# Two heads on one core: x transposed out of DRAM, state columns in chunk order

## The chip, the cores and the metric

The kernel runs on one core of a Trainium2 chip. The time is device microseconds of one execution; a kernel's time is the median of several. The profiled execution is one more run of the same program, with the hardware profiler on. Its *span* is the time from the first to the last instruction that the profile shows; the device time has about two microseconds more around it.

## The reference

Two independent parts read two inputs of 2048 tokens by 448 features (bf16); their outputs stand side by side in one array of 2048 x 896.

```
# A: dilated local attention, 16 heads of 28, window 8, dilation 2
q, k, v = split(x @ wqkv)                      # per head
idx     = pos[:, None] - 2 * arange(8)         # masked where negative
logits  = (q . k[idx]) * 28 ** -0.5
a       = (softmax(logits) . v[idx]) @ wo

# B: diagonal state model, 448 complex states
Bu = x @ B_bar.T                               # B_bar from Lambda, log_dt, B_re, B_im
h  = Lam_bar * h + Bu[t]                       # over t = 0 .. 2047
b  = 2 * real(h @ Cmat.T) + x * Dskip
out = concatenate([a, b], -1)
```

## The kernel before

All work is written as small operations (Python functions marked `@op`), and the string ORDER (lines 32 to 61) lists them one by one: this fixes the order on every engine by hand. A name is followed by its arguments; `@` gives the PSUM banks it takes; `.` means that its copy out of PSUM goes to ScalarE, `=` to VectorE. Capital names are mostly TensorE work (QS, QK, V_, BU, BR, UP, H_, DN, C, W_, AV, AL), small ones copies, vector work and DMA issues. Nearly all DMAs are issued by SyncE, in the order in which they stand in the program, so one that waits holds up all behind it.

**Layout.** TensorE contracts over partitions, so x is needed with features on partitions. 448 features are three full blocks of 128 and a half block of 64. The half blocks of two groups of tokens share one tile, one in partitions 0 to 63 and one in 64 to 127, and their two matmuls of half height run side by side. `part` (line 238) issues such a group: six matmuls of full height (k=0) or two of half height (k=1).

**Part A.** The tile `xT` holds x transposed: group 0 has tokens 0 to 1023, group 1 the rest, each as two halves of 512 tokens in seven blocks (three, the shared half block, three). Group 0 is loaded as rows into `xnA`, a view of `xbuf` (lines 141 to 144); TensorE transposes it with an identity (XI for tokens 0 to 511, XA and XH for 512 to 1023), and the copies xi, xa and xh bring it from PSUM into `xT`. Group 1 is loaded as rows too (line 157), in an order of columns that makes two token tiles fill seven whole blocks, and transposed by four DMAs from SBUF to SBUF (line 173). Weights come in slices (w_load, and w_half for the 64 rows of the half block). QS and QK make q and k, V_ makes v. P multiplies q with shifted k on VectorE, E_ sums heads on TensorE, lt copies the sums, TD transposes them by DMA, sma/smb/smc are the softmax. AL, ad and sp lay the weights out in a band (through DRAM), AV multiplies by v, W_ by wo, w copies the result into one of six `ya` buffers, ow stores it.

**Part B.** T=4 steps make a chunk, 512 chunks in all; chunks are of two kinds, even and odd. Rows of B_x are loaded early into `xnB` (x_load, line 164), again with shuffled columns, each quarter cb holding 128 chunks of one kind. xt(cb) transposes a quarter from SBUF to SBUF into `xTB`, which is `xbuf` again, once its A rows are done with. So columns of `xTB` stand sorted by kind: first all even chunks, then all odd ones. XR then loads B_x once more in plain order for the skip term. Bn holds B_re and B_im, BD transposes it into BT. BU multiplies; its sums for step j stay in PSUM, BR adds the rotated state of step j-1 (from the tile Z) on top of them, and z copies the sum to Z, or for the last step only the even half to Z3. UP adds the even chunks' end to the odd chunks', y copies that; sa, sb and sd run the scan over pairs of chunks; DN, H_ and their additions dn and h bring the scan's result back to each step, C multiplies by the output matrix, c adds the skip term and oc stores.

**Around the start.** WU warms TensorE with 22 small matmuls on zeros. SyncE issues the loads of lines 141 to 179 one after another, then what ORDER names.

Of the kernel before, what the change touches and what calls it, by code (L numbers as in the profile page):

```python
# [32 lines left out]
WU@0 XI0@0 xi00= xi01. XI1@1 XI2@2 xi10= xi11. PP@3 xi20. pcopy pa QS00@4 pb QS10@5 qk000. pd_ pc XH1@6 pe XA10@7  # L33
xh1. XA11@1 qk010. xa10= QK021@32 xa11. QK031@04 P000 ty0 QS01@6 pf QS11@5 P001 QK051@71 QK030 tf0 qk011. qk001. pg
ts00 QK050 qk031. ts10 ts20 QK020 qk051. P010 qk050. ty5 V_010@56 ty2 tf5 qk020. QK061@41 P011 V_001@73 ts05 V_011
V_000 v010. qk030. tf2 ts15 QK060 qk021= ts25 v000. P020 v001. QK040@50 qh001. rb2 v011. qh011. QK041 V_111@27 ty1
P021 V_101@36 V_110 qk040. qk041. tf1 ts02 E_00@50 P030 E_01 ts01 ts12 E_02 qh000. V_100 P031 qh010. v111. P040
QK130@41 ts22 ts11 v101. P041 v100. V_411@76 ts21 QK131 E_03 hc0 P050 ty6 E_04 ty4 V_410 qk131. tf6 qk130. QK100@31
P051 v411. ts06 v410. P060 QK110@46 ts16 BD v110. ts26 P061 QK101 ty3 QK151@72 QK111 qk100. E_05 rb0 qk101. E_06
qk110. QK150 tf4 lt00 P100 V_401@31 qk151. V_501@45 V_500 rb3 qk150. xt1 ts04 P101 lt01 QK120@27 ts14 qk111. tf3  # L40
v501. QK140@06 xt0 v500. P110 ts03 QK121 P111 QK141 qk120. QK161@54 V_400 qk140. xt3 P120 ts13 qk121. QK160 v400.
P121 qk141. v401. E_10@20 xt2 ts23 P130 E_11 ts24 V_510@73 qh101. P131 qh110. qh111. E_12 TD0 qh100. P140 E_13 hc1
V_511 P141 v511. v510. LC BU301@61 BU201@45 P150 BU300 sma0 BU200 OZ z30. XR BU400@37 z20. P151 smb0 BU000@64 P160
BR31 P161 BU001 ci1. BU401 E_14 z00. E_15 ci2= CD1 z40. E_16 rb1 z31. BR21 BR01 lt11 BU500@63 ci0= CD2 z21. smc0
z01. BU211@10 ci3. CD0 BU311@54 BU501 BU310 lt10 z50. CD3 BR32 BR41 BU210 z41. xd3 TD1 z32. BR51 xd2 BR22 AL0@2 z51.
BR33 z22. BU100@67 al0= z33. xd0 ca3 ad0 BU011@53 BU111@12 BU101 sma1 OP pm3 BU010 z10. pm0 wo UP3 AL1@6 cs3 smb1
BR11 xd1 BR02 BU110 z02. smc1 z11. BR03 al1. BR12 BU510@57 z03. ad1 z12. pm1 sp0 ca6 UP0 BR13 BU600@61 z13. y3. y0.
cs6 UP1 BR23 BU601 y1. z23. BU511 sa0 BU411@43 z60. BR52 pm4 ca1 BU410 sp1 sb0 BR61 z52. BR42 BU611@26 ca2 BU610 pm2
sd0 z61. AX@5 z42. BR53 BR62 AL2@1 ax= z53. z62. cs1 DN0@4 UP5 adx UP2 al2. DN1@5 BR43 dn0 BR63 y2. dn1 AL3@2 ad2
z63. sa2 H_10@1 y5. H_20@4 z43. H_11@0 al3. UP6 UP4 H_21@5 y6. H_00@7 ad3 y4. H_01@2 AV011@6 ca4 h21 spx AV010@3 h20  # L50
AV030@5 h01 av011. sp2 AV000@4 av010. cs2 AV020@6 av030. sb2 AV021@2 av000. AV001@3 av020. AV031@5 sd2 av001. W_00@4
sp3 av031. av021. W_20@6 ca5 h11 DN2@3 W_01@5 h00 DN3@2 dn2 w20. W_10@0 dn3 w01. sa4 ow20 W_11@7 ow01 W_21@3 w11.
w10. H_03@6 h10 H_02@2 w00. H_22@5 cs4 W_30@7 w21. ow00 sb4 H_23@0 ow21 H_13@1 w30. W_31@4 ow10 ca0 ow30 h13 AV100@3
ow11 h03 AV110@7 sd4 AV111@1 av110. AV131@6 av111. AV101@7 h02 av131. AV121@1 sa6 av101. AV130@6 av121. AV120@2 cs0
av130. DN5@7 av100. cs5 W_71@1 av120. dn5 W_61@6 w31. sb6 w71. h23 H_05@3 ow31 W_51@2 w61. ow71 ow61 W_41@7 w51= h05
H_15@4 ow51 H_25@1 W_50@0 h15 sd6 DN4@6 W_60@2 w50. w41. W_40@3 ow50 w60= ow41 DN6@4 C32@0 w40. ow60 dn6 dn4 ow40
h25 H_06@7 H_16@2 H_04@3 h06 H_12@4 H_14@6 h04 W_70@1 c32 H_24@7 C31@3 h22 oc32 w70= h12 C33@0 ow70 c31 h14 oc31
H_26@5 C30@1 c33 h26 oc33 h24 C02@4 c30 oc30 C20@3 c02 C00@6 c20 h16 oc20 CH0@0 c00 C01@5 oc00 C11@7 c01 ch0 oc01
C12@1 oh0 oc02 C13@4 C22@3 C03@2 c22 c12 oc22 c13 C21@6 oc12 c11 oc13 oc11 C10@5 c21 c03 oc21 CH1@0 oc03 c10 ch1
oc10 oh1  # L60
# [3 lines left out]
def kernel(  # L64
# [48 lines left out]
    def evict(e, o, i):  # L113
        (ACT.copy if e == "A" else V.tensor_copy)(o, i)  # L114
# [45 lines left out]
    xnB = keep.tile([128, 4, T, D], BF16, tag="xnB")  # L160
    xP = xnB.rearrange("p c j d -> p c (j d)").rearrange("p c (a n) -> p c a n", a=2)
    xB_r = B_x[0].rearrange("(q p h a b) d -> h p q a b d", q=2, p=128, h=2, a=2)

    def x_load(hh):
        for d0, d1, b, c in ((0, D, 0, 0), (D, 512, 1, 384), (512, 896, 1, 0)):
            for q in range(2):
                SP.dma_start(xP[:, 2 * hh + q, :, d0:d1], xB_r[hh, :, q, :, b, c:c + d1 - d0])
# [122 lines left out]
    @op  # L290
    def xi(h, k, e):
        p, c = pp["xi", h], 256 * h
        if h == 2:
            evict(e, xT[0:64, 0, 3], p[0:64, 0:512])
        elif k == 0:
            evict(e, xT[:, 0, 0:2, c:c + 256], p[:, 0:512].rearrange("p (f n) -> p f n", f=2))
        else:
            evict(e, xT[:, 0, 2, c:c + 256], p[:, 512:768])

    @op  # L300
    def XA(b, part):
        p = pp["xa", b, part] = ps(BF16)
        for t in range(4):
            for k, f in enumerate((0, 1) if part == 0 else (2,)):
                PE.transpose(p[:, 512 * k + 128 * t:512 * k + 128 * t + 128], xnA[:, 4 * b + t, 128 * f:128 * f + 128], ident[:])

    @op
    def xa(b, part, e):
        p = pp.pop(("xa", b, part))
        if part == 0:  # L310
            evict(e, xT[:, 0, 4 * b:4 * b + 2], p.rearrange("p (f n) -> p f n", f=2))
        else:
            evict(e, xT[:, 0, 4 * b + 2], p[:, 0:512])

    @op
    def XH(b):
        p = pp["xh", b] = ps(BF16)
        for t in range(4):
            PE.transpose(p[64 * b:64 * b + 64, 128 * t:128 * t + 128], xnA[:, 4 * b + t, 384:448], ident[:])

    @op
    def xh(b, e):
        r = slice(64 * b, 64 * b + 64)
        evict(e, xT[r, 0, 3], pp.pop(("xh", b))[r, 0:512])
# [595 lines left out]
```

## Time and profile before

| | us |
|---|---|
| median of 3 runs (132.54 to 133.14) | 133.01 |
| the profiled execution | 132.89 |
| its span | 130.7 |
| matmuls of line 244 with xT and wq, 512 columns (96) | 20.6 busy |
| matmuls of line 244 with BT (112) | 23.6 busy |
| products of line 379 on VectorE (24) | 28.7 busy |
| copies into Z on ScalarE (35) | 15.8 busy |

Busy time of a matmul counts its whole passage through the array, about 380 ns for 512 columns, while the next one starts after some 215 ns; the pace is therefore read from starts, or from the chain of waits, where a piece such as "0.43 PE ps L722 x2" is two matmuls one behind the other. In the page a line such as `ps<-Z,R` names the output tile and the operands. SPq and ACTq are the queues in which SyncE and ScalarE issue DMAs; the time shown there is the issuing, not the transfer.

SyncE's queue from 0.8 to 64 us holds the loads and transposes that the change is about (start, length in us, kind, tile written and tile read, how many):

```profile
0.81 0.45 SPq L141 DMA_DIRECT2D xbuf<-in_A_x_dram  x1
1.32 0.45 SPq L142 DMA_DIRECT2D xbuf<-in_A_x_dram  x1
1.82 1.04 SPq L128 DMA_DIRECT2D wq<-in_A_wqkv_dram  x2
2.91 0.69 SPq L144 DMA_DIRECT2D xbuf<-in_A_x_dram  x1
...
10.55 1.69 SPq L157 DMA_DIRECT2D xbuf<-in_A_x_dram  x3
12.29 4.54 SPq L167 DMA_DIRECT2D xnB<-in_B_x_dram  x6
17.94 5.35 SPq L173 DMA_TRANSPOSE xT<-xbuf  x4
...
26.04 4.51 SPq L167 DMA_DIRECT2D xnB<-in_B_x_dram  x6
31.11 5.15 SPq L672 DMA_TRANSPOSE BT<-Bn  x1
36.30 8.11 SPq L696 DMA_TRANSPOSE xbuf<-xnB  x4
44.46 1.86 SPq L413 DMA_TRANSPOSE attn<-lt  x1
```

### The profile page before, as it was taken

How to read it: one execution, taken by the hardware profiler on the slowest of the kernel's cores; microseconds unless marked ns; L12 is line 12 of the kernel's file. 1: busy time of each engine (PE TensorE's matmuls, PEld its weight loads, DVE VectorE, ACT ScalarE, POOL GpSimd, SP SyncE). 2: the span in 40 equal slices, each digit the busy share in tenths (PEclk: the TensorE clock that was granted, in tenths of full speed). 3: DMA queues.
4: the chain of work that ended last, by engine and by line, in shares of the span. 5: the costliest groups of instructions: out<-in, count | busy, mean ns of one | idle time of the engine just before them, and what ended most of it. 6: DMA issues, size and time to landing. Idle time of an engine off the chain costs nothing.

```text
span 130.7 us, 2869 instructions
## 1 busy us (share of the span) xinstructions
PE 125.4 (96%) x1067; PEld 62.2 (48%) x1067; DVE 113.4 (87%) x206; ACT 88.8 (68%) x185; POOL 19.8 (15%) x37
## 2 busy tenths in 40 slices
PE   6999999999999999999999999999899999999991
PEld 6543443434233334334454356854575555565550
DVE  5679999999999999999999899999997999752282
ACT  1779999999978996995979999997497300000000
POOL 6802000000000000200799920000000000000000
PEclk9999999999999999999999999999999999999999
DMA  3997989899999998999786999999412332213043
GB/s 116 238 207 174 326 230 167 197 197 258 139 259 210 212 200 187 310 303 209 209 200 222 185 169 293 255 179 185 141 54 70 105 105 94 87 55 103 0 146 118
DMA packets 47780, 23.24 MB, mean 178 GB/s; under 512 B 35639, under 2 KB 46711, under 8 KB 47767
## 3 DMA queue, kind: packets, MB, share of 16 engines
q1 hardware_dynamic: 47560, 23.03, 78.3%
q8 instruction: 8, 0.13, 0.4%
q10 hardware_dynamic: 207, 0.04, 0.2%
q14 instruction: 5, 0.04, 0.1%
HBM read 11.69 MB, written 6.37 MB: 138 GB/s over the span
## 4 chain that ended last, share of the span: by engine, by line
PE 80%; ACT 7%; DMA 6%; SPq 3%; issue 1%; DVE 0%; ACTq 0%
PE ps L244 38%; PE ps L807 15%; PE ps L547 6%; PE ps L534 5%; PE ps L391 5%; ACT ctmp L684 4%; DMA out_dram<-ya 3%; PE ps L722 3%; DMA wq<-in_A_wqkv_dram 3%; PE ps L788 3%; ACT Z L114 2%; SPq L128 2%; PE ps L348 1%; PE ps L827 1%; PE ps L395 1%
## 5 line engine op out<-in xcount | busy, mean ns | idle before, releaser
L379 DVE TENSOR_TENSOR pr<-qf,kf 128x2048 bf16<-128x2048 bf16 x24 | 28.7, 1236 | 0.1
L244 PE MATMUL ps<-xbuf,BT 128*128 128x512 bf16 (+1 forms) x112 | 23.6, 380 | 0.0
L244 PE MATMUL ps<-xT,wq 128*128 128x512 bf16 (+1 forms) x96 | 20.6, 380 | 0.1
L807 PE MATMUL ps<-Cw,Z 128*128 128x448 bf16 x105 | 20.5, 352 | 0.0
L114 ACT CAST Z<-ps 128x512 bf16<-128x512 f32 (+1 forms) x35 | 15.8, 520 | 3.0 <-PE ps L722 1.5
L813 DVE TENSOR_TENSOR xbuf<-ps,xnB 128x448 bf16<-128x448 f32 x15 | 9.0, 620 | 7.6 <-PE ps L807 7.5
L244 PEld LDWEIGHTS <-BT 128*128 128x128 bf16 (+1 forms) x112 | 8.9, 97 | 12.6 <-issue 3.5
L807 PEld LDWEIGHTS <-Z 128*128 128x128 bf16 x105 | 10.3, 98 | 9.4
L793 DVE TENSOR_TENSOR Z<-ps,Z 128x512 bf16<-128x512 f32 x21 | 13.7, 680 | 0.2 <-PE ps L788 0.2
L547 PE MATMUL ps<-wo,oT 128*128 128x448 bf16 x64 | 13.6, 353 | 0.0
L244 PEld LDWEIGHTS <-wq 128*128 128x128 bf16 (+1 forms) x96 | 7.8, 97 | 11.0 <-issue 2.3
L244 PE MATMUL ps<-wq,xT 128*128 128x448 bf16 (+1 forms) x64 | 13.0, 354 | 0.0
L877 POOL MEMSET PT<- 128x4320 f32 x3 | 11.0, 3698 | 7.2 <-DVE xnB L797 7.2
L114 ACT CAST ya<-ps 128x448 bf16<-128x448 f32 (+1 forms) x14 | 7.0, 566 | 5.5 <-PE ps L547 2.8
L684 ACT ACTIVATE ctmp<-Cw,c2t 64x448 f32<-64x448 bf16 x14 | 9.3, 667 | 0.3
L547 PEld LDWEIGHTS <-oT 128*128 128x128 bf16 x64 | 6.2, 98 | 5.7 <-ACT oT L114 0.2
L534 PE MATMUL ps<-PT,v_s 128*32 128x135 bf16 (+1 forms) x256 | 8.8, 298 | 0.0
L114 ACT CAST oT<-ps 128x512 bf16<-128x512 f32 x17 | 8.7, 620 | 0.1
L244 PEld LDWEIGHTS <-xT 128*128 128x128 bf16 (+1 forms) x64 | 4.8, 97 | 7.5 <-issue 4.1
L114 ACT CAST v_s<-ps 128x448 bf16<-128x448 f32 x16 | 8.2, 542 | 0.1
L534 PEld LDWEIGHTS <-v_s 128*32 128x32 bf16 x256 | 7.0, 110 | 0.7 <-ACT Z L114 0.4
L114 ACT CAST kf<-ps 128x512 bf16<-128x512 f32 x12 | 6.7, 582 | 0.7 <-PE ps L244 0.7
(150 smaller groups left out, 180.9 us busy)
## 6 DMA issues: line engine op xcount, KB each, us to landing
PT<-pd SPq DMA_DIRECT2D x16, 156.0 KB, 5.2
xnB<-in_B_x_dram SPq DMA_DIRECT2D x2, 896.0 KB
out_dram<-ya SPq DMA_DIRECT2D x16, 112.0 KB, 1.7
out_dram<-xbuf SPq DMA_DIRECT2D x15, 112.0 KB, 1.7
pd<-Ak SPq DMA_DIRECT2D x2, 640.0 KB, 3.5
xbuf<-in_A_x_dram SPq DMA_DIRECT2D x2, 448.0 KB
xnB<-in_B_x_dram SPq DMA_DIRECT2D x4, 224.0 KB, 5.4
xnB<-in_B_x_dram SPq DMA_DIRECT2D x4, 192.0 KB, 4.0
```

The lines of the kernel that those rows point to most:

```text
L114: (ACT.copy if e == "A" else V.tensor_copy)(o, i)
L244: PE.matmul(o, l, r, start=(first and i == 0), stop=(not first and i == len(pairs) - 1 and not more[s]))
L379: V.tensor_tensor(t[:], q.unsqueeze(1).to_broadcast((128, 4, 512)), k4, ALU.mult)
L391: PE.matmul(acc[s][32 * i:32 * i + 32], E[:, f, ws, :], t[:, i, :], start=(f == 0 and ws == 0), stop=False)
L534: PE.matmul(p[32 * hh:32 * hh + 32, 128 * bl:128 * bl + n], v_s[:, t, 4 * hg + hh, :], PT[:, t % NS, (4 * hg + hh) // HS, (4 * hg + hh) % ...
L547: PE.matmul(p[:, 0:D], late["oT"][:, b // 4, hg, par, 128 * (b % 4):128 * (b % 4) + 128], late["wo"][:, hg, :], start=(hg == 0), stop=(hg ...
L684: ACT.activation(t[a:a + 64, 0:D], Cw[b:b + 64, g, :], ACTF.Copy, scale=c2t[a:a + 64, g:g + 1])
L722: PE.matmul(pp["z", g, j][:], rot(g, 0), late["Z"][:, g, j - 1, :], start=False, stop=True)
L793: V.tensor_tensor(zz, pp.pop(("h", j, g))[:], zz, ALU.add)
L807: PE.matmul(p[:, 0:D], z, Cw[:, g, :], start=(g == 0), stop=(g == G - 1))
L813: V.tensor_tensor(yo, pp.pop(("c", j, ct))[:, 0:D], xnB[:, ct, j, :], ALU.add)
L877: POOL.memset(late["PT"][:, 4 * i:4 * i + 4].rearrange("p t g n -> p (t g n)").bitcast(F32), 0.0)
```

## The change

- Only tokens 0 to 511 of A are still loaded as rows and transposed by TensorE. The operations XA, xa, XH and xh are gone, as are the shuffled row loads of A's second group and of B_x and the transposes from SBUF to SBUF.
- t_load transposes 512 rows by 512 columns straight out of DRAM. The half block is now the first 64 features, not the last. For the first half of a group (s=0) two DMAs bring three blocks and one block; for the second (s=1) one DMA brings four blocks that start 64 columns early, so that the 64 features come to lie in partitions 64 to 127. A needs four such DMAs, B six (xt is now by step j, each over all 512 chunks).
- `xTB` therefore has its columns in chunk order, and so have the sums in PSUM. Z and Z3 stay sorted by kind: z and y read PSUM at a step of two (by_kind), and BR and UP write it at a step of two.
- Tiles are placed anew: `xbuf` holds only xTB (and later `yob`, the output buffers of c), while `xnA` and `Bn` lie in `xnB`, before XR fills it. The second half-row load of the weights goes out on ScalarE's queue.
- ORDER is written anew throughout.

```
-    xbuf = keep.tile([128, NT * D], BF16, tag="xbuf")
-    xnA = xbuf.rearrange("p (t d) -> p t d", d=D)
+    xbuf = keep.tile([128, 16 * 512], BF16, tag="xbuf")
+    yob = xbuf[:, 0:8 * D].rearrange("p (t d) -> p t d", d=D)
+    xnB = keep.tile([128, 4, T, D], BF16, tag="xnB")
+    xn = xnB.rearrange("p c j d -> p (c j d)")
+    xnA = xn[:, 0:8 * D].rearrange("p (t d) -> p t d", d=D)
+    Bn = xn[:, 8 * D:].rearrange("p (g d) -> p g d", d=512)
...
     w_half(0, 0, 128, 0, D, eng=ACT)
+    w_half(1, 0, D, 0, D, eng=ACT)
     SP.dma_start(xnA[:, 0:2], xA_r[:, 0:2])
     SP.dma_start(xnA[:, 2:4], xA_r[:, 2:4])
+    xT = s2.tile([128, 2, 8, 512], BF16, tag="xT")
+
+    def t_load(x, off, row, n, out, s):
+
+        for b, k, c in (((1, 3, 64), (0, 1, 0)), ((4, 4, -64),))[s]:
+            SP.dma_start(out[:, b:b + k], bass.AP(x.tensor, x.offset + off + c, [[row, n], [1, 128 * k]]), transpose=True)
+
     w_load(0, 128, 0, D)
-    SP.dma_start(xnA[:, 4:8], xA_r[:, 4:8])
-    w_half(1, 0, 256, 0, D)
+    t_load(A_x, 512 * D, D, 512, xT[:, 0], 1)
     w_load(128, 128, 0, D)
-    w_half(0, 128, 128, 0, D)
+    w_half(0, 128, 320, 0, D)
     w_load(256, 192, 0, D)
-    for s in range(2):
-        w_half(s, 256, 192, 0, D)
     w_load(0, D, 2 * D)
     for s in range(2):
         w_half(s, 0, D, 2 * D)
-    for d0, d1, b, c in ((0, D, 8, 0), (D, 512, 12, 384), (512, 896, 12, 0)):
-        SP.dma_start(xA1[:, :, d0:d1], xA_r[:, b:b + 4, c:c + d1 - d0])
-    x_load(0)
-    for t in range(4):
-        SP.dma_start(xT[:, 1, :, 128 * t:128 * t + 128], xA1[:, t], transpose=True)
+    t_load(A_x, 1024 * D, D, 512, xT[:, 1], 0)
+    t_load(A_x, 1536 * D, D, 512, xT[:, 1], 1)
...
-    def xt(cb):
-
-        SP.dma_start(xTB[:, :, :, 128 * cb:128 * cb + 128].rearrange("p a b c -> p (a b) c"),
-                     xnB[:, cb].rearrange("p j d -> p (j d)"), transpose=True)
+    def xt(j):
+
+        t_load(B_x, j * D, T * D, NC, xTB[:, j // 2], j % 2)
...
+    def by_kind(p):
+
+        return p.rearrange("p (c h) -> p h c", h=2)
...
     def BR(g, j):
-        PE.matmul(pp["z", g, j][:], rot(g, 0), late["Z"][:, g, j - 1, :], start=False, stop=True)
+        PE.matmul(by_kind(pp["z", g, j]), rot(g, 0), late["Z"][:, g, j - 1].rearrange("p (h c) -> p h c", h=2), start=False, stop=True)
...
-            evict(e, late["Z"][:, g, j, :], pp.pop(("z", g, j))[:])
+            evict(e, late["Z"][:, g, j].rearrange("p (h c) -> p h c", h=2), by_kind(pp.pop(("z", g, j))))
         else:
-            evict(e, late["Z3"][:, g, EV:EV + N2], pp["z", g, j][:, 0:N2])
+            evict(e, late["Z3"][:, g, EV:EV + N2], by_kind(pp["z", g, j])[:, 0])
...
     def UP(g):
-        PE.matmul(pp["z", g, T - 1][:, N2:], rot(g, T - 1), late["Z3"][:, g, EV:EV + N2], start=False, stop=True, skip_group_check=True)
+        PE.matmul(by_kind(pp["z", g, T - 1])[:, 1], rot(g, T - 1), late["Z3"][:, g, EV:EV + N2], start=False, stop=True, skip_group_check=True)
```

The first lines of ORDER, before and after:

```
-WU@0 XI0@0 xi00= xi01. XI1@1 XI2@2 xi10= xi11. PP@3 xi20. pcopy pa QS00@4 pb QS10@5 qk000. pd_ pc XH1@6 pe XA10@7
-xh1. XA11@1 qk010. xa10= QK021@32 xa11. QK031@04 P000 ty0 QS01@6 pf QS11@5 P001 QK051@71 QK030 tf0 qk011. qk001. pg
+WU@0 XI0@0 xi00= xi01. XI1@1 XI2@2 xi10= xi11. PP@3 xi20. QS00@4 pcopy pa pb QS10@5 pd_ pc pe ty0 QS01@6 ty5 qk000.
+tf0 QS11@7 qk010. pf tf5 QK021@01 QK051@32 QK031@45 QK030 P000 ts00 P001 QK020 qk011. qk030. pg qk001. QK050 ts10
```

More of the change, by code (lines that the diff above doesn't have):

```diff
@@ L32 @@
 ORDER = """
-WU@0 XI0@0 xi00= xi01. XI1@1 XI2@2 xi10= xi11. PP@3 xi20. pcopy pa QS00@4 pb QS10@5 qk000. pd_ pc XH1@6 pe XA10@7
-xh1. XA11@1 qk010. xa10= QK021@32 xa11. QK031@04 P000 ty0 QS01@6 pf QS11@5 P001 QK051@71 QK030 tf0 qk011. qk001. pg
-ts00 QK050 qk031. ts10 ts20 QK020 qk051. P010 qk050. ty5 V_010@56 ty2 tf5 qk020. QK061@41 P011 V_001@73 ts05 V_011
-V_000 v010. qk030. tf2 ts15 QK060 qk021= ts25 v000. P020 v001. QK040@50 qh001. rb2 v011. qh011. QK041 V_111@27 ty1
-P021 V_101@36 V_110 qk040. qk041. tf1 ts02 E_00@50 P030 E_01 ts01 ts12 E_02 qh000. V_100 P031 qh010. v111. P040
@@ L38 @@
[L38 to L57, printed above, removed]
@@ L58 @@
-H_26@5 C30@1 c33 h26 oc33 h24 C02@4 c30 oc30 C20@3 c02 C00@6 c20 h16 oc20 CH0@0 c00 C01@5 oc00 C11@7 c01 ch0 oc01
-C12@1 oh0 oc02 C13@4 C22@3 C03@2 c22 c12 oc22 c13 C21@6 oc12 c11 oc13 oc11 C10@5 c21 c03 oc21 CH1@0 oc03 c10 ch1
-oc10 oh1
+WU@0 XI0@0 xi00= xi01. XI1@1 XI2@2 xi10= xi11. PP@3 xi20. QS00@4 pcopy pa pb QS10@5 pd_ pc pe ty0 QS01@6 ty5 qk000.
+tf0 QS11@7 qk010. pf tf5 QK021@01 QK051@32 QK031@45 QK030 P000 ts00 P001 QK020 qk011. qk030. pg qk001. QK050 ts10
+qk020. ts20 V_000@74 qk031. qk051. qk021= ts05 V_010@60 rb0 qk050. ts15 rb3 ty2 V_011 QK041@52 ts25 V_001 V_101@13
@@ new lines @@
+v010. QK040 tf2 v011. ty1 P010 v000. V_100 v001. rb2 ts02 qk040. V_110@60 xt1 qk041. tf1 v100. V_411@74 P011 ts12
+QK061@52 v101. V_111 QK060 xt2 v111. P020 ts01 ts11 V_410 ts22 P021 qh011. v110. QK110@13 ty6 qh000= xt0 ts21 tf6
+qh001. E_00@06 v411. P030 E_01 v410. E_02 qh010. QK111 P031 ty4 QK101@54 QK131@72 qk111. xt3 QK100 ts06 P040 ts16
+ts26 QK130 qk110. tf4 BD ty3 P041 hc0 QK120@31 qk101. qk130. P050 ts04 QK150@47 ts14 qk100. tf3 qk131. QK121 P051
+QK151 qk121. V_501@52 LC E_03 ts03 E_04 P060 qk120. E_05 qk150. V_500 ts13 P061 ts23 qk151. V_510@13 P100 v500. ts24
@@ new lines @@
+v501. E_06 P101 QK140@47 lt00 lt01 P110 ci0. QK141 TD0 V_401@52 V_511 P111 QK161@06 V_400 v511. qk141. CD0 P120 ci3.
+QK160 v510. XR ci2= qk140. P121 BU200@37 v401. qh110. sma0 ci1. BU300@14 CD3 qh100. qh101. BU201 CD1 BU301 P130
+E_10@20 OZ z20. z30. E_11 qh111. BR21 CD2 P131 BR31 v400. BU000@31 hc1 smb0 P140 BU400@65 P141 E_12 z21. P150 E_13
+z31. E_14 ca6 BU401 P151 BU001 BU501@74 BU500 z00. P160 z40. ca3 BR01 P161 BU210@36 rb1 z01. E_15 z50. E_16 cs6 BR51
+lt10 xd1 BU310@17 lt11 z51. smc0 TD1 BU101@20 BU211 BU311 BR22 BR41 BR32 BU100 z41. z22. z32. BU010@45 z10. cs3 OP
@@ new lines @@
+pm3 sma1 BR11 BU011 z11. pm0 BU111@31 AL0@2 BR33 BR02 al0. xd3 BU110 z02. ad0 smb1 wo xd2 BR03 BR12 AL1@0 z12. smc1
+BU600@24 al1. pm1 z33. ad1 z03. BR13 BR23 sp0 BU601 z13. z23. UP3 UP0 z60. UP1 BU410@30 y1. y0. y3. sa0 ca2 BU510@21
+pm4 sp1 ca4 BU411 sb0 BU511 BU611@57 BR61 BR52 BR42 pm2 cs4 BU610 z52. z61. sd0 z42. BR53 BR62 AX@2 z53. AL2@4 z62.
+cs2 DN0@3 ax. BR43 UP2 al2. dn0 DN1@5 UP5 adx BR63 dn1 y2. AL3@2 ad2 y5. H_21@3 sa2 z43. H_01@4 z63. H_10@5 al3.
+H_00@6 UP6 UP4 H_20@1 y6. ad3 AV030@2 y4. h10 ca1 spx AV001@7 h00 AV000@0 h20 AV031@5 sp2 av030. AV010@6 sb2 av000.
@@ new lines @@
+AV020@1 av010. AV021@2 av020. sd2 AV011@0 av021. H_11@6 av011. W_00@1 sp3 av031. av001= W_30@2 h21 DN2@0 DN3@5
+W_21@7 w30. h11 ca0 dn2 W_31@3 ow30 dn3 cs1 W_20@2 h01 W_01@6 w20. sa4 w00. H_02@0 ow20 H_13@5 w31. H_03@4 H_23@2
+w01. W_10@1 ow31 ca5 h13 H_22@3 W_11@6 sb4 w21. AV131@5 w11. h02 ow21 AV100@7 av131. ow11 xd0 AV120@6 w10. ow00
+AV101@0 ow10 av120. sd4 AV111@5 ow01 av101. AV121@1 av100. AV110@6 av111. cs0 av121. AV130@0 sa6 av110. DN5@7 H_12@5
+av130. DN4@1 W_61@6 h22 W_50@0 h12 sb6 W_51@3 dn4 W_41@5 dn5 w51. sd6 W_40@1 w41. h03 H_14@7 W_60@3 w40. cs5 w50.
@@ L61 @@
+DN6@5 H_24@4 w61= w60. ow50 H_04@1 C32@0 h04 ow61 h14 H_05@3 dn6 C33@6 h23 h05 C31@1 h24 c33 c32 H_06@7 oc33 H_26@5
+H_15@2 h06 H_25@3 H_16@4 c31 C30@6 h26 oc31 h25 W_71@0 c30 C01@7 oc30 ow40 ow41 C02@1 ow51 C03@5 c02 W_70@3 c03 w71.
+h15 C22@6 w70. ow71 h16 ow70 C21@1 c22 c01 oc22 C00@5 oc03 oc01 oc02 C13@0 oc32 ow60 CH0@2 c13 C20@3 oc13 C10@4 c20
+oc20 C12@6 c10 c21 oc10 c00 C11@7 oc21 ch0 oc00 c12 oh0 CH1@0 c11 oc12 ch1 oc11 oh1
 """
@@ L117 @@
     V.memset(wz[:], 0.0)
-    xbuf = keep.tile([128, NT * D], BF16, tag="xbuf")
-    xnA = xbuf.rearrange("p (t d) -> p t d", d=D)
+    xbuf = keep.tile([128, 16 * 512], BF16, tag="xbuf")
[4 more added lines that the diff above has]
+    Bn = xn[:, 8 * D:].rearrange("p (g d) -> p g d", d=512)
     xA_r = A_x[0].rearrange("(t p) d -> p t d", p=128)
     wq = s2.tile([128, 4, 3 * D], BF16, tag="wq")
-    wq_r = A_wqkv[0:384].rearrange("(f p) n -> p f n", p=128)
+    wq_r = A_wqkv[64:448].rearrange("(f p) n -> p f n", p=128)
     def w_load(c, n, *at):
@@ L132, in w_half @@
         o, i = (bass.AP(t.tensor, t.offset + c + at[0], [list(t.ap[0]), [D, len(at)], [1, n]])
-                for t in (wq[64 * s:64 * s + 64, 3], A_wqkv[384:448]))
+                for t in (wq[64 * s:64 * s + 64, 3], A_wqkv[0:64]))
         eng.dma_start(o, i)
@@ L153 @@
         w_half(s, 0, D, 2 * D)
-    xA1 = xbuf[:, 8 * D:].rearrange("p (t n) -> p t n", n=2 * D)
-    for d0, d1, b, c in ((0, D, 8, 0), (D, 512, 12, 384), (512, 896, 12, 0)):
-        SP.dma_start(xA1[:, :, d0:d1], xA_r[:, b:b + 4, c:c + d1 - d0])
[L160 to L167, printed above, removed]
-    x_load(0)
-    xT = s2.tile([128, 2, 7, 512], BF16, tag="xT")
-    for t in range(4):
-        SP.dma_start(xT[:, 1, :, 128 * t:128 * t + 128], xA1[:, t], transpose=True)
-    Bn = s2.tile([128, G, 512], BF16, tag="Bn")
-    for d0, d1, c in ((0, D, 0), (D, 512, 384)):
+    t_load(A_x, 1024 * D, D, 512, xT[:, 1], 0)
+    t_load(A_x, 1536 * D, D, 512, xT[:, 1], 1)
+    for d0, d1 in ((64, 512), (0, 64)):
         for ri, b in enumerate((B_B_re, B_B_im)):
-            SP.dma_start(Bn[64 * ri:64 * ri + 64, :, d0:d1], b[:, c:D].rearrange("(g p) d -> p g d", p=64))
-    x_load(1)
+            SP.dma_start(Bn[64 * ri:64 * ri + 64, :, d0:d1], b[:, 0:d1 - d0].rearrange("(g p) d -> p g d", p=64))
     dsk = const.tile([128, D], BF16, tag="dsk")
@@ L283, in XI @@
             for t in range(4):
-                PE.transpose(p[0:64, 128 * t:128 * t + 128], xnA[:, t, 384:448], ident[:])
+                PE.transpose(p[0:64, 128 * t:128 * t + 128], xnA[:, t, 0:64], ident[:])
             return
@@ L287, in XI @@
             for f in range(3):
-                PE.transpose(p[:, 256 * f + 128 * t:256 * f + 128 * t + 128], xnA[:, 2 * h + t, 128 * f:128 * f + 128], ident[:])
+                PE.transpose(p[:, 256 * f + 128 * t:256 * f + 128 * t + 128],
+                             xnA[:, 2 * h + t, 64 + 128 * f:192 + 128 * f], ident[:])
     @op
@@ L293, in xi @@
         if h == 2:
-            evict(e, xT[0:64, 0, 3], p[0:64, 0:512])
+            evict(e, xT[0:64, 0, 0], p[0:64, 0:512])
         elif k == 0:
-            evict(e, xT[:, 0, 0:2, c:c + 256], p[:, 0:512].rearrange("p (f n) -> p f n", f=2))
+            evict(e, xT[:, 0, 1:3, c:c + 256], p[:, 0:512].rearrange("p (f n) -> p f n", f=2))
         else:
[L298 to L324, printed above, removed]
+            evict(e, xT[:, 0, 3, c:c + 256], p[:, 512:768])
     def wqk(m, rows, kt):
@@ L337, in QK @@
         part(("qk", u, m), k,
-             [[(p[s][:], wqk(m, slice(64 * s, 64 * s + 64), 3), xT[64 * s:64 * s + 64, u, 3]) for s in range(2)]] if k else
-             [[(p[s][:], wqk(m, slice(0, 128), kt), xT[:, u, 4 * s + kt]) for s in range(2)]
+             [[(p[s][:], wqk(m, slice(64 * s, 64 * s + 64), 3), xT[64 * s:64 * s + 64, u, 4 * s]) for s in range(2)]] if k else
+             [[(p[s][:], wqk(m, slice(0, 128), kt), xT[:, u, 4 * s + 1 + kt]) for s in range(2)]
               for kt in range(3)])
@@ L347, in QS @@
         for kt in range(3):
-            PE.matmul(p[:], wqk(m, slice(0, 128), kt), xT[:, 0, 4 * s + kt], start=(kt == 0), stop=False)
-        PE.matmul(p[:], wqk(m, slice(64 * s, 64 * s + 64), 3), xT[64 * s:64 * s + 64, 0, 3], start=False, stop=True)
+            PE.matmul(p[:], wqk(m, slice(0, 128), kt), xT[:, 0, 4 * s + 1 + kt], start=(kt == 0), stop=False)
+        PE.matmul(p[:], wqk(m, slice(64 * s, 64 * s + 64), 3), xT[64 * s:64 * s + 64, 0, 4 * s], start=False, stop=True)
     @op
@@ L511, in V_ @@
         part(("v", b0, par), k,
-             [[(p[s][:, 0:D], xT[64 * s:64 * s + 64, b0 // 4, 3, c + par:c + 256:2], wq[64 * s:64 * s + 64, 3, 2 * D:3 * D])
+             [[(p[s][:, 0:D], xT[64 * s:64 * s + 64, b0 // 4, 4 * s, c + par:c + 256:2], wq[64 * s:64 * s + 64, 3, 2 * D:3 * D])
                for s in range(2)]] if k else
-             [[(p[s][:, 0:D], xT[:, b0 // 4, 4 * s + kt, c + par:c + 256:2], wq[:, kt, 2 * D:3 * D])
+             [[(p[s][:, 0:D], xT[:, b0 // 4, 4 * s + 1 + kt, c + par:c + 256:2], wq[:, kt, 2 * D:3 * D])
                for s in range(2)] for kt in range(3)])
@@ L646, in tf @@
     def tf(g):
-        kM, fr = keep.tile([128, N2], F32, tag="kM", name="kM")[:], pp["fr", g][:]
+        kM, fr = s2.tile([128, N2], F32, tag="kM", name="kM")[:], pp["fr", g][:]
         V.tensor_scalar(kM, iot[:], fT[:, g:g + 1], MAGIC, ALU.mult, ALU.add)
@@ L688, in cs @@
         V.scalar_tensor_tensor(Cw[:, g, :], Cw[:, g, :], c1t[:, g:g + 1], pp["ctmp", g][:, 0:D], ALU.mult, ALU.add)
-    xTB = xbuf.rearrange("p (a b c) -> p a b c", a=2, b=7)
+    xTB = xbuf.rearrange("p (a b c) -> p a b c", a=2, c=512)
     @op
-    def xt(cb):
-        SP.dma_start(xTB[:, :, :, 128 * cb:128 * cb + 128].rearrange("p a b c -> p (a b) c"),
-                     xnB[:, cb].rearrange("p j d -> p (j d)"), transpose=True)
+    def xt(j):
+        t_load(B_x, j * D, T * D, NC, xTB[:, j // 2], j % 2)
     @op
@@ L712, in BU @@
         part(("bu", g, jp), k,
-             [[(p[s][:], BT[64 * s:64 * s + 64, g, 3, :], xTB[64 * s:64 * s + 64, jp, 3, :]) for s in range(2)]] if k else
-             [[(p[s][:], BT[:, g, f, :], xTB[:, jp, 4 * s + f, :]) for s in range(2)] for f in range(3)],
+             [[(p[s][:], BT[64 * s:64 * s + 64, g, 0, :], xTB[64 * s:64 * s + 64, jp, 4 * s, :]) for s in range(2)]] if k else
+             [[(p[s][:], BT[:, g, 1 + f, :], xTB[:, jp, 4 * s + 1 + f, :]) for s in range(2)] for f in range(3)],
              more=(jp == 1, True))
+    def by_kind(p):
+        return p.rearrange("p (c h) -> p h c", h=2)
     def rot(g, k):
@@ L727, in z @@
         if j < T - 1:
-            evict(e, late["Z"][:, g, j, :], pp.pop(("z", g, j))[:])
+            evict(e, late["Z"][:, g, j].rearrange("p (h c) -> p h c", h=2), by_kind(pp.pop(("z", g, j))))
         else:
-            evict(e, late["Z3"][:, g, EV:EV + N2], pp["z", g, j][:, 0:N2])
+            evict(e, late["Z3"][:, g, EV:EV + N2], by_kind(pp["z", g, j])[:, 0])
     @op
     def UP(g):
-        PE.matmul(pp["z", g, T - 1][:, N2:], rot(g, T - 1), late["Z3"][:, g, EV:EV + N2], start=False, stop=True, skip_group_check=True)
+        PE.matmul(by_kind(pp["z", g, T - 1])[:, 1], rot(g, T - 1), late["Z3"][:, g, EV:EV + N2], start=False, stop=True, skip_group_check=True)
     @op
     def y(g, e):
-        evict(e, late["Z3"][:, g, OD:OD + N2], pp.pop(("z", g, T - 1))[:, N2:])
+        evict(e, late["Z3"][:, g, OD:OD + N2], by_kind(pp.pop(("z", g, T - 1)))[:, 1])
     def scan_args(g0):
@@ L810, in c @@
     def c(j, ct):
-        yo = pp["yo", j, ct] = xnA[:, late["m"] % 8]
+        yo = pp["yo", j, ct] = yob[:, late["m"] % 8]
         late["m"] += 1
@@ L833, in ch @@
         if i == 0:
-            pp["yo"] = xnA[:, late["m"] % 8]
+            pp["yo"] = yob[:, late["m"] % 8]
             late["m"] += 1
```

## The prediction

> **What bounds the kernel now.** I read the page first, then the chain of waits, then the busy time by stretch.
>
> ```profile
> PE 125.4 (96%) x1067; PEld 62.2 (48%) x1067; DVE 113.4 (87%) x206; ACT 88.8 (68%) x185; POOL 19.8 (15%) x37
> PE 80%; ACT 7%; DMA 6%; SPq 3%; issue 1%; DVE 0%; ACTq 0%
> ...
> 5.60 3.69 DMA wq<-in_A_wqkv_dram
> 9.29 0.05 issue
> 9.33 0.61 PE ps L244 x4
> ...
> 12.09 11.82 PE ps L244 x62
> ...
> 90.00:96.00 6.00, 5.28 (x110) 3.43 (x111) 5.88 (x13) 3.94 (x8) 0.00 (x0) 1.00 0.56 149
> ```
>
> The first line is busy time by engine, the second the shares of the chain that ended last, the next the chain in order of time (start, length, what), the last one stretch (PE, PEld, DVE, ACT, POOL, granted clock, DMA share, GB/s). From 12.09 us to the last matmul (about 127.8) TensorE hardly stops: the stretches between have it idle for 0.06, 0.04 and 0.72 us. Its matmuls run at stream pace (8 in 1.49 us for a group of six whole and two half-height ones), so the span is close to a sum of matmul columns. Before 12.09 the chain is SyncE's issuing and then a weight load. VectorE, at 5.7 to 6.0 of 6.0 us in most stretches from 24 to 96, is second.
>
> So three things count: matmul work removed, the pace of the matmuls that are changed, and how soon TensorE's stream starts. A transfer saved later is worth nothing unless TensorE waits for it.
>
> **The start.** Removed from TensorE are the 16 transposes of XH1, XA10 and XA11. They run from 8.02 to 9.20, and QS01 and QS11, which need them, from 9.87. By 12.09 TensorE has done the four QS and the four half-height matmuls of QK021 and QK031. In their place one transposing DMA brings tokens 512 to 1023 from DRAM, 512 tokens by four blocks of 128 features: 16 blocks of 128x128. No row shows a transpose out of DRAM; those out of SBUF are
>
> ```profile
> xT<-xbuf SPq DMA_TRANSPOSE x4, 3.4
> xbuf<-xnB SPq DMA_TRANSPOSE x4, 4.7
> BT<-Bn SPq DMA_TRANSPOSE x1, 7.2
> ```
>
> with 7, 14 and 28 blocks, the last number being us from issue to landing. That is 2.1 + 0.18 a block, so 5.0 us for 16. SyncE reaches it at 2.91 (the two x loads and two weight loads ahead of it keep their places), so it lands near 8.0. QS01 and QS11 then take 8.0 to about 9.9 (two of them took 1.9 to 2.2 before). The issue itself takes SyncE about 2.5 us (2.03 for 14 blocks, 5.15 for 28), against 1.43 for the x load and the half-row load it stands for. The next two weight loads go out from 5.4 to 6.5 instead of 4.43 to 5.55, and the half-row load of columns 128 to 447 after them at 6.6; with 3.6 us to landing that is 10.2. The half-height QK matmuls start there and reach at 10.8 where they were at 12.09: **1.2 us gained**. The other bound: if a block from DRAM costs double, landing is at 10.9, the same work ends near 13.3, and the start loses 1.2. I take -1.0, nearer the rows of the same instruction.
>
> VectorE loses the 0.69 us copy xa10 ahead of its first P000, ScalarE two copies of 0.58, so they can follow. The second half-row load moves to ScalarE's queue, about 0.7 us ahead of its table load at 2.85; ScalarE sat idle 0.68 us before its first copy at 5.03, which covers it. Without that cover QS00 would be some 0.7 later; it is in the upper end.
>
> **The middle's transfers.** From SyncE go the x loads (0.69 + 1.69 us of issuing), the twelve loads of B_x (4.54 + 4.51), three half-row loads (about 2.0), and the SBUF transposes (5.35 + 8.11): 26.9 us. Added are ten transposes out of DRAM, 48 blocks for A and 64 for B, at 0.145 to 0.186 a block: 16 to 21 us. SyncE gets to Cr, dsk and the softmax transposes 6 to 11 us sooner. I cost this at nothing, since no TensorE wait between 12 and 72 us comes from them. The second half of A's tokens is issued at about 10 to 16 and lands by 19 (before: 18 to 23.3, plus 3.4); the new order wants it in V_411, after some 11 us of QK and V work, at 21 or later. At double the price a block it would come near 23, a wait of up to 2 us. XR, which rewrites the tile that now also holds Bn, waits for BT's transpose on SyncE with four Cw transposes behind it; before it waited at the same place for the transposes of x. Copying kM, yob and Bn to other places changes no instruction's size.
>
> **The state model's sums.** Columns now stand in the order of chunks, and the two kinds alternate. The 21 matmuls of BR and the seven of UP therefore write every second fp32 word of their bank, and the copies z and y read every second word. The copies are covered by a row: lt already reads PSUM at a step of two words, 597 ns in the median, against 586 for Z. No more than 0.4 us of ScalarE in all. For a matmul that writes lone words the trace has no row. Around it are
>
> ```profile
> 23.90 1.48 PE ps L391 x24
> 59.98 0.43 PE ps L722 x2
> 62.14 0.06 PE ps L461 x2
> 80.91 2.07 PE ps L534 x63
> ```
>
> L722 is BR now: 215 ns for 512 columns, 0.42 ns a column, and UP takes 0.11 us. L461 (AL) writes PSUM in runs of four words with gaps: 64 columns in 29 ns, 0.45 a column, so gaps between runs cost nothing. That is the lower bound, **0**. L391 and L534 are both four matmuls side by side in strips of 32 columns. L391 reads its moving operand word after word, 62 ns each or 0.48 ns a column for the four; L534 reads at a step of four elements, 33 ns each, 0.97 ns a column for its 135. So the row with lone elements runs at half the pace, though it is a read and near a floor for short matmuls. That gives the upper bound: 21 x 0.215 + 7 x 0.11 = **5.3 us**. I take this end: BR's words stand alone as in L534, and in L461 each has its neighbour.
>
> The Trainium skill ("PSUM — Partial Sum Buffer", Specifications) gives PSUM lines of 8 bytes, two fp32 values, and says that any non-contiguous pattern slows matmuls significantly. L461 shows that "any" is too strong here, but its runs fill whole lines, and BR's don't. It names no factor; by that rule the sum would stand above the lower bound, and without it at the lower bound.
>
> All 28 lie between 53 and 80 us, where TensorE is idle 0.1 us, so nothing absorbs it. VectorE then waits for TensorE, not the reverse.
>
> **The new order.** It moves ca, W and AV steps against each other. At 93 us TensorE lost 0.72 us since ScalarE's copy of ya waited 2.0 us for an output transfer and then ran two ca. If TensorE comes 4 us later, those transfers have landed: -0.4. A bad order could cost as much as it did here, so 0 to -0.7 in the gain and +0.7 at worst. The tail (last matmul, a 0.39 copy, one store) keeps its 2.9 us.
>
> **Sum.** The profiled execution took 132.89 us with a span of 130.7, and stands 0.1 below the median of 133.01. 132.89 - 1.0 + 5.3 - 0.4 = **136.8**. Its own range is 135.0 (start gains the full 1.2 and the order 0.7, price 4.0 us) to 138.5 (start gains nothing).
>
> **Rivals.**
> 1. *Strided writes are free.* For it: L461 at full pace, and lt's copies. Against: neither is a lone word written by TensorE. Then only the start and the order count: 132.89 - 1.0 - 0.3 = **131.6**, faster. It decides as soon as BR runs at 0.22 us a piece.
> 2. *The transposes out of DRAM are slow, strided writes free.* Rows of 1024 bytes are read at a step of 896 (A) or 3584 (B) bytes, which no row shows. At double the block price the start loses 1.2 and V_411 up to 2: about **134.6**. Against: the 448 KB x load took the same 5.1 us from issue to use (2.91 to 8.02) as I give the transpose.
> 3. *A price in between*, as where two half-rate writes overlap the next weight load: 2.6 us, giving **134.1**.
>
> **Chances.** Forecast 0.52, rival 1 0.34, rival 2 0.08, rival 3 0.06. A measurement of this kernel can tell about 0.5%, so "same" is 132.35 to 133.67. Rival 1 is faster in 0.30 of its 0.34, else the same; rivals 2 and 3 put 0.03 into "same" and the rest into slower; a sliver of the forecast's (0.01) falls to "same". That makes 0.30 / 0.08 / 0.62. The range must reach to rival 1 to leave out no more than two in ten: 131.0 to 138.4 leaves out some 0.08 below and 0.05 above. The likeliest case's own range is 135.0 to 138.5.
>
> **What would show it.** BR's starts 0.43 us apart and UP's 0.21 would show the price; 0.215 and 0.11 refute it, and with it the forecast. QS01 starting near 8.0 shows the start; at 10 or later, rival 2. The transposes' issue-to-landing near 5 us for 16 blocks shows the block price. TensorE's end at about 131.5 in the span, with idle after 12 us still under 1 us, shows that the price fell on the path; if idle there grows by 2 us or more, I missed a wait.

## The result, and the profile after

The changed kernel takes 142.47 us in the median (141.79 to 143.51) against 133.07 for the kernel before on the same chip: ratio 1.072, interval 1.065 to 1.079. The forecast was slower, 136.8 us; the slowdown is 9.4 us where 3.8 were forecast, and the time lies above the range (131.0 to 138.4). The profiled execution took 143.51 us with a span of 141.6, the upper end of the runs shown, so the span below is about a microsecond more than the median's.

From the page of the changed kernel, TensorE's busy tenths and its granted clock in 40 slices of 3.54 us:

```profile
PE   7989999999998979639999999999999999999991
...
PEclk9999999999999999995999999999999999999999
```

TensorE, which was at 9 in all but one of the slices between the first and the last, is thinner from 42 us on, has a hole in the slices from 57 to 64 us (digits 6 and 3), and in the slice after it, from 64 us, the granted clock is at half (digit 5). The stretches show the hole in numbers (PE, PEld, DVE, ACT, POOL busy, granted clock, DMA share, GB/s):

```profile
42.00:48.00 6.00, 5.28 (x28) 2.06 (x25) 4.87 (x10) 3.69 (x7) 0.11 (x1) 1.00 0.66 143
48.00:54.00 6.00, 5.20 (x33) 1.78 (x34) 4.84 (x5) 5.82 (x11) 0.00 (x0) 1.00 0.87 263
54.00:60.00 6.00, 4.86 (x43) 1.75 (x41) 5.07 (x5) 2.77 (x4) 0.84 (x1) 1.00 0.96 158
60.00:66.00 6.00, 3.38 (x14) 0.92 (x14) 4.27 (x8) 4.81 (x8) 0.00 (x0) 0.77 0.00 0
```

From 42 to 66 us TensorE is idle for 5.3 us, where the kernel before had it busy throughout; its last stretch there reads

```profile
60.00:66.00 6.00, 6.00 (x44) 2.71 (x43) 5.90 (x10) 4.34 (x8) 3.18 (x1) 1.00 0.89 214
```

The largest piece, 3.5 us, ends at 62.4; of the rest, 1.5 us lie before 54 in shorter waits, the two longest for copies on ScalarE (0.7 and 0.5 us). The chain of waits names the cause of the largest piece (start, length, what):

```profile
53.95 6.28 DMA Cw<-Cn
...
60.39 0.67 ACT ctmp L650
...
61.76 0.59 ACT Z L113
...
62.40 0.59 PE ps L691
```

ScalarE's instruction at line 650 is ca6. It waits for the last of the four transposes into Cw, which lands at 60.2, and behind it in ScalarE's queue stand the copies of BU's sums into Z. TensorE's next BR needs one of them. SyncE's queue shows what is ahead of that transpose:

```profile
45.27 1.22 SPq L643 DMA_TRANSPOSE Cw<-Cn  x1
...
47.21 0.91 SPq L670 DMA_DIRECT2D xnB<-in_B_x_dram  x2
48.21 8.52 SPq L643 DMA_TRANSPOSE Cw<-Cn  x3
```

XR's load of 1.8 MB goes out at 47.2, and the three transposes behind it take 8.5 us to issue. In the kernel before they stood behind XR too, but ScalarE came to the first ca only at 63.3:

```profile
54.69 6.40 SPq L677 DMA_TRANSPOSE Cw<-Cn  x4
```

The matmuls that write at a step of two words, from the chain:

```profile
75.03 0.86 PE ps L691 x2
...
80.93 0.75 PE ps L703 x3
```

BR (line 691) comes at 0.43 us and UP (line 703) at 0.22 to 0.25, against 0.215 and 0.11 before. The start, from the instructions in order of time on TensorE:

```profile
8.66 0.81 PE L314 MATMUL ps<-xT,wq 128*128 128x512 bf16 x2 [0.65 <-DMA xT<-in_A_x_dram]
...
10.47 0.39 PE L315 MATMUL ps<-xT,wq 64*128 64x512 bf16 x1
```

QS01 starts at 8.66 and the four QS are through at 10.9. The first full-height matmul of QK stands behind the same work in both kernels, four QS and the half-height matmuls of three QK. It starts at 11.44, and at 12.23 in the kernel before.

### The profile page after: what moved, and what is told of

Same layout as the page of the kernel before. It is cut to its first block, busy times and chain, and to the rows that moved or that the text cites. A ratio compares the mean times of both kernels' runs of the same rounds, so it can differ in the third digit from the quotient of the medians.

```text
span 141.6 us, 2791 instructions
## 1 busy us (share of the span) xinstructions
PE 130.6 (92%) x1042; PEld 62.9 (44%) x1051; DVE 111.7 (79%) x202; ACT 90.4 (64%) x186; POOL 19.7 (14%) x37
## 4 chain that ended last, share of the span: by engine, by line
PE 55%; DMA 4%; ACT 3%; DVE 2%; issue 1%; ACTq 0%
PE ps L776 14%; PE ps L235 12%; PE ps L513 9%; PE ps L691 6%; PE ps L500 6%; DMA Cw<-Cn 4%; PE ps L757 3%; DVE pr L345 2%; PE ps L703 1%; PE ps L796 1%; PE ps L357 1%; ACT ctmp L650 1%; PE ps L427 1%; PE ps L744 1%; ACT Cn L113 1%
## 5 line engine op out<-in xcount | busy, mean ns | idle before, releaser
L235 PE MATMUL ps<-xbuf,BT 128*128 128x512 bf16 (+1 forms) x108 | 24.9, 390 | 1.1 <-ACT v_s L113 0.5
L235 PEld LDWEIGHTS <-BT 128*128 128x128 bf16 (+1 forms) x112 | 9.6, 102 | 20.4 <-issue 12.8
L113 ACT CAST ya<-ps 128x448 bf16<-128x448 f32 (+1 forms) x16 | 8.0, 541 | 16.1 <-DMA out_dram<-ya 12.2
L691 PE MATMUL ps<-Z,R 128*128 128x512 bf16 x20 | 10.5, 612 | 3.5 <-ACT Z L113 3.5
L113 ACT CAST oT<-ps 128x512 bf16<-128x512 f32 x16 | 8.2, 600 | 0.1
L235 PEld LDWEIGHTS <-xT 128*128 128x128 bf16 (+1 forms) x64 | 5.4, 97 | 6.3 <-issue 1.6
L357 PE MATMUL ps<-pr,E 128*32 128x512 bf16 x96 | 6.7, 401 | 0.7 <-ACT kh L113 0.7
```

What stands on the lines that cost most here:

```text
L235: PE.matmul(o, l, r, start=(first and i == 0), stop=(not first and i == len(pairs) - 1 and not more[s]))
L357: PE.matmul(acc[s][32 * i:32 * i + 32], E[:, f, ws, :], t[:, i, :], start=(f == 0 and ws == 0), stop=False)
L691: PE.matmul(by_kind(pp["z", g, j]), rot(g, 0), late["Z"][:, g, j - 1].rearrange("p (h c) -> p h c", h=2), start=False, stop=True)
```

## The experiments

Two things were to be told apart: the price of the strided writes, and the hole in the middle. Theory 1 has them as two costs with different causes; theory 2 has the slow BR open the hole as well.

### The strided writes by themselves, in the kernel before

BR and UP of the kernel before, with another order of the output words and nothing else changed; the sums land in the wrong columns.

```
 def BR(g, j):
-    PE.matmul(pp["z", g, j][:], rot(g, 0), late["Z"][:, g, j - 1, :], start=False, stop=True)
+    PE.matmul(pp["z", g, j].rearrange("p (c h) -> p h c", h=2), rot(g, 0), late["Z"][:, g, j - 1].rearrange("p (h c) -> p h c", h=2), start=False, stop=True)
```

UP takes the second half of the same view. Expected of this run:

> The kernel before with one thing changed: BR and UP write every second word of PSUM, in two passes, with the same number of words (the sums are then added to the wrong columns). Theory 1: BR 0.43 us apart, UP 0.21, and 5.3 us on the span: 138.3 us. Theory 2: more than 5.3, since a stall follows, 140 or more. If ScalarE or VectorE set the middle, less: 134 to 136.

Measured: 137.73 us, ratio 1.036 (1.030 to 1.042), so 4.8 us with an interval of 4.0 to 5.5. Two pieces of its chain:

```profile
62.12 0.86 PE ps L722 x2
...
76.31 0.22 PE ps L734
```

The second kernel leaves two words out after each two, with the view `"p (c h w) -> p h c w", h=2, w=2`:

> The kernel before with BR and UP writing two words, leaving two out, and so on (the sums are added to the wrong columns). If a lone word costs half a line of 8 bytes: full pace, BR 0.215 us apart, 133.0 us. If any gap in the output costs: BR 0.43 us apart or something between, 135 to 138 us.

Measured: 133.12 us, ratio 0.999 (0.996 to 1.002), no change. Its chain has

```profile
60.47 0.43 PE ps L722 x2
...
66.73 0.11 PE ps L734
```

So half the pace belongs to lone words; gaps between pairs of words cost nothing. Theory 1's price is shown, and no stall of its own follows from it in the kernel before.

### ca later in the changed kernel (run e2)

```
-E_14 ca6 BU401 ... z40. ca3 BR01 ... E_16 cs6 BR51
+E_14 BU401 ... z40. BR01 ... E_16 BR51
...
-z22. z32. BU010@45 z10. cs3 OP pm3 sma1 BR11 BU011 z11. pm0 BU111@31 AL0@2 BR33 BR02 al0. xd3 BU110
+z22. z32. ca3 BU010@45 z10. cs3 OP pm3 sma1 BR11 BU011 z11. ca6 pm0 BU111@31 AL0@2 BR33 BR02 al0. xd3 cs6 BU110
```

> The changed kernel with ca6, ca3 and cs6 moved some 10 us later in ORDER, behind the landing of Cw; the strided writes stay. Theory 1: the stall of TensorE between 54 and 66 us goes, 138 to 139 us. Theory 2 (the slow BR is behind the stall): no more than 1 us better, 141.5 or more.

Measured: 137.94 us, ratio 1.037 (1.031 to 1.042), 4.5 us better than the change. BR still takes 0.43 us; the stretch of the hole is full and the clock is whole:

```profile
54.00:60.00 6.00, 5.95 (x53) 2.12 (x52) 5.11 (x5) 4.14 (x7) 0.84 (x1) 1.00 0.80 123
60.00:66.00 6.00, 6.00 (x46) 2.01 (x39) 3.88 (x6) 3.08 (x6) 4.93 (x2) 1.00 0.23 44
```

### XR behind the transposes into Cw (run e5)

In the next run ca stays early; only the load that was ahead of three of the transposes moves behind them.

```
-QK160 v510. XR ci2= qk140. ... E_11 qh111. BR21 CD2 P131
+QK160 v510. ci2= qk140. ... E_11 qh111. BR21 CD2 XR P131
```

> The changed kernel with XR (1.8 MB of B_x and dsk) issued behind the four Cw transposes and not between them; ca6 keeps its early place. If the Cw transposes are late since they share the DMA engines with XR's load: Cw lands by 54 instead of 60.2, ca6 doesn't wait, the stall shrinks to under 1 us and the time to 138 to 139.5 us. If they are late since their own copies or SyncE's issuing are late: Cw lands at 57 or later and the time stays above 141.

Measured: 137.54 us, ratio 1.036 (1.031 to 1.041), 4.9 us better than the change. SyncE's queue of this run:

```profile
43.76 7.19 SPq L643 DMA_TRANSPOSE Cw<-Cn  x4
...
51.68 0.90 SPq L670 DMA_DIRECT2D xnB<-in_B_x_dram  x2
```

Each of the four now takes 1.19 to 1.25 us to issue (1.22 to 3.89 in the change; the rest of the 7.2 us are waits for their copies), and 2.9 us after its issue the last has landed, before 53. The first ca runs at 55.3 without waiting for Cw. So the hole has one place and two ways out: ca was asked for before Cw could be there, and Cw was late since the large load went out ahead of three of its four transposes. Whether they then waited behind it in the queue or shared the DMA engines with it, no run tells apart.

### Rows by kind of chunk, first try

B is transposed by kind, so that BR, UP, z and y use whole rows again (by_kind becomes a split into halves).

```
 def xt(j):
-    t_load(B_x, j * D, T * D, NC, xTB[:, j // 2], j % 2)
+    for h in range(2):
+        t_load(B_x, (j + T * h) * D, 2 * T * D, N2, xTB[:, j // 2, :, N2 * h:N2 * h + N2], j % 2)
 def by_kind(p):
-    return p.rearrange("p (c h) -> p h c", h=2)
+    return p.rearrange("p (h c) -> p h c", h=2)
```

> The changed kernel with B's transposes out of DRAM split by kind of chunk (twelve DMAs of 256 rows where there were six of 512), so that BR, UP, z and y use whole rows of PSUM again. Theory 1 (two separate costs: writes of lone words at half pace, 5.3 us, and a stall of some 4 us between 42 and 66 us where ScalarE waits for Cw): BR starts 0.215 us apart again, the stall stays, 137.2 us. Theory 2 (the slow BR sets off the stall as well): the stall goes with it, 133 us or less. If the writes cost nothing, 142.5.

Measured: 145.69 us, ratio 1.092 (1.085 to 1.098): worse than the change, as neither theory had it. The queues tell why:

```profile
21.00 18.77 SPq L155 DMA_TRANSPOSE xbuf<-in_B_x_dram  x12
...
44.77 0.59 SPq L259 DMA_DIRECT2D Cr<-in_B_C_re_dram  x1
```

Twelve transposes hold SyncE for 18.8 us where six took 12.5, so Cr is asked for 6.8 us later (37.96 before). ScalarE's copy ci0 waits 8.8 us for it, with copies of v behind it that free banks, and TensorE stands still from 45.6 to 52.05. The run doesn't tell the theories apart: it puts a new wait of the same kind in place of the price that it takes away. The wait at ca6 is in its trace as well, 3.4 us.

### Rows by kind, with SyncE's queue set right

As above, with the order xt1, xt0, BD, LC, xt2, TD0, xt3 on SyncE, and three places for ca and XR: ca late as in e2 (run e6); ca early and XR behind Cw (e7); ca early and XR ahead, as in the change (e8).

```
-V_110@60 xt1 qk041. tf1 v100. ... QK060 xt2 v111. ... V_410 ... qh000= xt0 ts21 ... xt3 QK100 ... BD ty3 ... LC E_03 ... TD0 V_401@52 V_511
+V_110@60 xt1 qk041. tf1 xt0 v100. ... QK060 v111. ... BD V_410 ... qh000= ts21 ... QK100 ... LC qk110. tf4 ty3 ... xt2 E_05 ... TD0 V_401@52 xt3 V_511
```

> The changed kernel with B transposed by kind of chunk (BR, UP, z, y on whole rows), ca6, ca3 and cs6 late as in e2, and SyncE's order such that BT and the first two steps of x come before the last two (xt1, xt0, BD, LC, xt2, TD0, xt3). Theory 1 (two prices, and a start that gains 1 us): BU200 no longer waits for BT as in the first run by kind, no stall over 1 us, 132.0 us, between 131.3 and 133.2. If the transposes out of DRAM cost something else in the middle: 134 or more.

> The changed kernel with B transposed by kind of chunk, SyncE's order of e6, ca6, ca3 and cs6 at their early places of the change, and XR behind the Cw transposes as in e5. Theory 1: neither price is paid, 132.0 to 133.0 us, better than e6, since ca then falls where ScalarE has time. If the early ca costs something of itself: 135 or more.

> As e7, but XR at its place in the change, ahead of three of the Cw transposes: rows written whole, and ca6 early. The first run by kind mixed this with a late BT. Theory 1: the stall at ca6 is there without the strided writes, some 4 to 6 us over e6 and e7: 137 to 139 us. If the stall needs the strided writes: 134 or less.

Measured, in this order: 134.20 (ratio 1.009, 1.007 to 1.012), 133.13 (0.998, 0.995 to 1.002) and 142.21 (1.067, 1.061 to 1.074). The first lies beyond its expected 131.3 to 133.2, and the second just above its 132.0 to 133.0. From 12 to 126 us TensorE is idle for 3.2 us in the first and 1.8 in the second, and for 0.8 in the kernel before; so what the start gains is spent again. The longest waits in the first are 0.9 us of AV for the weights that come through the band and 0.8 us of BR for a copy into Z.

The second against the third is the hole without the strided writes: 9.1 us, where 4 to 6 were expected. What waited for whom in the third (engine, line, releaser: total, times, longest):

```profile
PE ps L689 <- ACT Z L110: 6.9, 1, 6.9
ACT ctmp L647 <- DMA Cw<-Cn: 6.8, 1, 6.8
```

And its stretch after the hole:

```profile
60.00:66.00 6.00, 2.75 (x7) 0.84 (x6) 3.27 (x6) 4.65 (x8) 0.00 (x0) 0.50 0.14 31
```

Theory 2 falls: the hole is there with whole rows. Four kernels make a square:

| median us | XR ahead of Cw | XR behind Cw |
|---|---|---|
| lone words | 142.47 (the change) | 137.54 |
| whole rows | 142.21 | 133.13 |

The second row differs from the first in more than the writes: it has twelve x transposes for six, in another order on SyncE.

The two costs don't add up. Cw lands at a time that SyncE's queue and the transfers set, 60.2 in the change and 61.2 with whole rows. A TensorE that gets there sooner only waits longer: ca6 waits 3.6 us in the one and 6.8 in the other. And after the idle stretch TensorE runs at the lower clock, with a mean of 0.77 in the stretch from 60 to 66 us in the one and 0.50 in the other.

### One try at beating both

In the better of the three TensorE was still idle 0.43 us between 54 and 60. The last two x transposes went behind Cw as well (xt3 just ahead of XR).

> As e7, with the last pair of x transposes (xt3) behind the four Cw transposes as well, ahead of XR. If what is left of the wait at ca6 (TensorE idle 0.43 us between 54 and 60) is Cw's landing at 54.3: Cw lands near 51.5, that idle goes, 132.3 to 132.9 us. If BU210 then waits for xt3: 133.5 or more.

Measured: 133.49 us, ratio 1.001 (0.999 to 1.004). Cw has landed when ca6 comes, and yet the time didn't fall: TensorE's idle time between 54 and 60 went only from 0.43 to 0.33 us, and in the stretch from 78 to 84 it rose from 0.68 to 1.03. The timeline has two new waits:

```profile
60.90 1.09 DVE L764 TENSOR_TENSOR xnB<-xnB,dsk 128x1792 bf16<-128x1792 bf16 x1 [1.51 <-DMA xnB<-in_B_x_dram]
...
79.09 0.27 PE L742 MATMUL ps<-Z,R 128*128 128x256 bf16 x1 [0.98 <-DVE Z L737]
```

VectorE waits 1.5 us for XR's load (0.4 with xt3 ahead of Cw), and TensorE's first DN waits 1.0 us for VectorE's scan (0.3 there). The chain of waits leads from the one to the other through VectorE, which is busy for 5.0 to 5.9 of 6.0 us in each stretch between 60 and 84. So no version here beats the kernel before; the best equal it.

## Why the prediction was wrong, point by point

- **The strided writes** were right: "21 x 0.215 + 7 x 0.11 = 5.3 us", each at half pace. The kernel before with them alone lost 4.8 us (4.0 to 5.5), and with XR behind Cw whole rows are 4.4 us better. The rule of the Trainium skill ("PSUM — Partial Sum Buffer", Specifications) was too strong in its word "any": pairs of words run at full pace, as its lines of two fp32 values would have it. The factor of two was read off L534, which reads at a step and doesn't write; that it came out exactly was in part luck.
- **The copies** that read at a step of two cost nothing: z takes 588 ns, 590 before.
- **The start** was nearly right: "1.2 us gained", taken as 1.0. The transpose of 16 blocks landed at 8.6, 5.2 us after its issue, 5.0 forecast. It was issued at 3.45 and not at 2.91, so QS01 started at 8.66 and not near 8.0, and the gain is about 0.8. In the trace SyncE waits 0.6 us there for one of the loads of x into xnA to land, a wait that the forecast didn't have.
- **The new order** is the step that failed: "A bad order could cost as much as it did here, so 0 to -0.7 in the gain and +0.7 at worst." The early ca, with XR ahead of Cw, cost 4.5 to 4.9 us, and 9.1 with whole rows. I treated the moved ca as work on ScalarE and not as a wait with a queue behind it. The rows to see it were there: in the kernel before, the transposes into Cw issue from 54.69 to 61.1 behind XR, and the first ca runs at 63.3. The new ORDER puts ca6 right after E_14, which ran at 54.4 in the kernel before, with BU's copies behind it.
- **The middle's transfers**, "I cost this at nothing", failed with it. It rested on TensorE having no wait on a transfer there, which held for the old order alone. The ten transposes out of DRAM held SyncE for 22.5 us where 16 to 21 were forecast. SyncE did get to Cr sooner (37.96, 46.37 before), and this was worth nothing, as XR's load still went ahead of three of the four transposes.
- **"TensorE's end at about 131.5 in the span, with idle after 12 us still under 1 us"** was the mark that I set, and "if idle there grows by 2 us or more, I missed a wait": it grew by over 5.
- **The rivals.** Free strided writes and a price in between are refuted by BR at 0.43 us. Slow transposes out of DRAM are refuted as I put them, since the 16 blocks landed within 0.2 us of what the rows from SBUF gave; but the number of transposes matters, as the first try by kind shows.

The sum by what was measured: 133.1 - 0.8 + 4.8 makes 137.1, and the kernel with XR moved took 137.5; the hole adds 4.9 to that. The 0.4 us between is left to the rest of the order; no run takes it apart.

## What to carry to other kernels

A step that is moved ahead on an in-order engine is to be checked by its inputs: write down when each lands by the queue that brings it, and what stands behind it on its engine. A small transfer that somebody waits for goes ahead of a large one that nobody needs yet. When two causes end in one wait for a transfer, taking one away shows nothing; take away both before a cost is called small.

## What the runs showed that was not expected

- A matmul that writes every second fp32 word of PSUM takes twice the time (0.43 us for 512 columns); with pairs of words and gaps of two it takes 0.215.
- Issuing a transposing DMA took SyncE no less than 1.2 us in these runs (1.19 to 1.25 for the 7 blocks of a Cw transpose, 1.28 in the median of the twelve by kind, of 2 to 8 blocks), and up to 3.9 for those 7 blocks with a large load ahead. Splitting six into twelve cost 6.3 us of SyncE.
- After TensorE had stood still for 3.5 us its matmuls ran at half pace for a while: in the changed kernel two BU matmuls at 64.11 took 1.06 us, where two of that size take 0.6 otherwise (0.215 to the second's start and 0.38 for it). Between 12 and 126 us the granted clock fell to half in the three kernels in which TensorE stood still there for over 3 us, and in no other.
